# Gated linear attention and a GELU feed-forward: late state products in four corners of the array

## The chip, the cores and the metric

The kernel runs on one core of one Trainium2 chip. The metric is device time in microseconds (us) of one execution. TensorE (PE) multiplies matrices and loads their stationary operand with a separate instruction (PEld in the profile); VectorE (DVE) and ScalarE (ACT) do elementwise work; GpSimd (POOL) does some of it and issues DMAs; SyncE (SP) only issues DMAs. Matmuls write to PSUM, a memory of 128 partitions and eight banks; everything else lives in SBUF.

## The reference

A gated linear attention runs over 4 batches, 8 heads and 768 steps with 48 values per head, and its result goes through a feed-forward layer:

```python
for t in range(S):
    state = alpha[:, :, t, :, None] * state + np.einsum('bhd,bhe->bhde', k[:, :, t], v[:, :, t])
    y[:, :, t] = np.einsum('bhd,bhde->bhe', q[:, :, t], state)
x = y.transpose(0, 2, 1, 3).reshape(3072, 384)
h = x @ w_in                                    # 384 x 2048
out = (0.5 * h * (1 + erf(h / sqrt(2)))) @ w_out  # 2048 x 384
```

## The kernel before

**Tiling.** The 3072 rows are cut into 12 groups of 256 steps (`NG`), three per batch. Attention of a group is done in two units, u = 0 and 1 (`NU`), so there are 24 units. A unit holds four heads: i = 0, 1 picks a pair, and h = 0, 1 picks the head of the pair, which sits in partitions 0 to 47 (h = 0) or 64 to 111 (h = 1). Its 256 steps are four chunks of 64 steps, j = 0 to 3, also written j = 2c + b. Even chunks (b = 0) and odd chunks (b = 1) have separate PSUM banks: the tile `ybank` is 128 partitions by 2 banks, the second index is b.

**A unit in order.** `ahead` (L247) makes decay products on DVE and scales q and k. `scores` (L284) and `turned` (L293) multiply q with k and transpose k; `turned_out` and `masked` take these out of PSUM. `inside` (L322, L340) adds to `ybank` each chunk's own part of the result and each chunk's new state. `chain` (L359) adds the states up from chunk to chunk on DVE. `outside_part` (L384) then adds to the result in `ybank` the product of each chunk's starting state with its q: 16 small products of 48 partitions by 48 columns against 64 steps, for every chunk, pair and head. A unit that begins a batch has no starting state for j = 0 and does 12 of the 16. Then `x_high` (L426) takes the result out on ACT, rounded to fp32r, and `x_low` (L430) writes the remainder on DVE; both go through `x_parts` (L409), which yields for each instruction its source in `ybank` and its two targets. For u = 0 that is one part, for u = 1 two (one into the tile `z`, which `spread` then copies into the last rows of `x` by six DMAs on SP's queue, and one into `x`).

**Where the small products lie in the array.** The partitions of the inputs fix the half of the array's rows that a product uses, and the partitions of the output fix the half of its columns. In `outside_part` both are given by h: `r` is used for `states`, for `qt` and for `ybank`. `scores` uses row half h with column half b and bank h; the first loop of `inside` uses row half b with column half h and bank b.

**Early and late units.** Groups 0 to 2 (`g < NSB`) are early: their feed-forward runs while the weights are still being converted, and their remainders are made by TensorE (`x_minus`, L435) in place. The other nine groups are late: 18 units, six of which begin a batch (groups 3, 6 and 9).

**Feed-forward.** For every group and each of eight slices f, `gemm1` (L457, 18 matmuls) fills `hp`, `gelus` (L469, L470) runs on ACT, `gelu_low` (L475) on DVE, and `gemm2` (L496, 12 matmuls) adds to `acc`; `evacuate` copies `acc` out at the end of a group.

**The order.** Nothing is reordered at run time: the order on PE, DVE, ACT and SP is laid down beforehand by a small planner (L608 to L885). Each step is an `Op` with an engine, a cost from the table `COST`, the steps that it depends on and a rank; the planner runs through time and takes for each free engine the ready step of lowest rank. A step that frees or fills a buffer is simply one of the dependences. Late `scores`, `inside` and `outer` (the step that calls `outside_part`) may be taken only `MARGIN` = 1.5 us after their inputs are ready in the plan, or when no feed-forward step can run, so PE fills with feed-forward work in between. In `plan_unit`, `xh` depends on `outer`, `xl` on `xh`, and the next unit's `inside` on both, since it overwrites `ybank`:

```python
    scan=1.62, back=2.05, q=1.35, qv=0.62, scores=1.2, kn=0.6, mask=0.62, inside=1.2, chain=1.15, outer=0.85, carry=0.26,
    xh=0.6, xl=0.65, spread=0.62, check=0.95, load=0.46, fetch=0.46, u=0.92, c0=0.56, c1=0.9, c2=0.45, c3=0.95, c4=0.92,
```

Of the kernel before, what the change touches and what calls it, by code (L numbers as in the profile page):

```python
# [33 lines left out]
    xh=0.6, xl=0.65, spread=0.62, check=0.95, load=0.46, fetch=0.46, u=0.92, c0=0.56, c1=0.9, c2=0.45, c3=0.95, c4=0.92,  # L34
    hi=0.84, lo=0.9, gemm1=2.12, gelu=0.58, minus=0.35, low=0.63, gemm2=2.1, part=1.1,
# [5 lines left out]
def gla_then_gelu_ffn(ctx: ExitStack, tc: tile.TileContext, q, k, v, alpha, akq, w_in, w_out, out):  # L41
    nc = tc.nc
    B, H, D, S = q.shape
# [5 lines left out]
    CS = C // 2  # L49
    NCH = G // CS  # L50
# [251 lines left out]
    def masked(g, u):  # L302
# [6 lines left out]
            op=ALU.mult,  # L309
        )  # L310

    def inside(g, u):
        d = cur[g, u]
        vn = vbuf[g % NB]
        for i in range(2):
            for j in range(NCH):
                c, b = j // 2, j % 2
                r, t = slice(b * CS, (b + 1) * CS), (2 * i + c) * CS
                for h in range(2):
                    o = slice(h * DP, (h + 1) * DP)  # L320
                    e = (4 * u + 2 * i + h) * D
                    nc.tensor.matmul(  # L322
                        ybank[o, b, t : t + CS],
                        lhsT=vn[r, c, e : e + DP],
                        rhs=d["ss"][r, h, 2 * i + c, :],
                        start=(i == 0 and c == 0),
                        stop=(j == 0 and g % GPB == 0),
                        skip_group_check=True,
                    )
        for j in range(NCH):  # L330
            if ends_batch(g, j):
                continue
            c, b = j // 2, j % 2
            r = slice(b * CS, (b + 1) * CS)
            for i in range(2):
                t = 2 * C + (2 * i + c) * D
                for h in range(2):
                    o = slice(h * DP, (h + 1) * DP)
                    e = (4 * u + 2 * i + h) * D
                    nc.tensor.matmul(  # L340
                        ybank[o, b, t : t + D],
                        lhsT=d["kn"][r, i, c * P + h * DP : c * P + (h + 1) * DP],
                        rhs=vn[r, c, e : e + D],
                        start=False,
                        stop=True,
                        skip_group_check=True,
                    )
# [24 lines left out]

    def outside_part(g, u):
        d = cur[g, u]
        for jj in range(NCH):
            for i in range(2):
                for h in range(2):
                    j = jj ^ h
                    if g % GPB == 0 and j == 0:
                        continue  # L380
                    r = slice(h * DP, h * DP + D)
                    c, b = j // 2, j % 2
                    t = (2 * i + c) * CS
                    ins = nc.tensor.matmul(  # L384
                        ybank[r, b, t : t + CS],
                        lhsT=states[u][j][r, i],
                        rhs=d["qt"][r, i, j * CS : (j + 1) * CS],
                        start=False,
                        stop=True,
                        skip_group_check=True,  # L390
                    )
                    tc.add_manual_dep(
                        ins.ins,
                        d["chain"].ins.name,
                        mybir.DependencyInfo(mybir.DependencyClass.Sync, mybir.DependencyReason.DATA),
                        reason="row tiles of one bank",
                    )
# [11 lines left out]
    def x_parts(g, u):  # L409
        x = cur[g, "x"]  # L410
        y = ybank[:, :, : 2 * C].rearrange("p b (i c t) -> p i c b t", c=2, t=CS)
        if 2 * u + 2 <= NK:
            parts = [(x[:, 2 * u : 2 * u + 2], y)]
        else:
            parts = [(cur[g, "z"].unsqueeze(1), y[:, 1:]), (x[:, NK - 1 : NK], y[:, :1])]
        for to, src in parts:
            hi, lo = (to[:, :, i].rearrange("p i (c b t) -> p i c b t", b=2, t=CS) for i in range(2))
            yield src, hi, lo

    def x_high(g, u):  # L420
        if u == 0:
# [6 lines left out]
    def x_low(g, u):  # L428
        for y, hi, lo in x_parts(g, u):
            nc.vector.tensor_tensor(out=lo, in0=y, in1=hi.bitcast(F32), op=ALU.subtract)  # L430
# [206 lines left out]
    def op(*args, **kw):  # L637
        ops.append(Op(*args, **kw))
        return ops[-1]
# [4 lines left out]
    def plan_unit(n):  # L644
        g, u = divmod(n, NU)
        d = unit[n] = {}
        p, pp_ = unit.get(n - 1, {}), unit.get(n - 2, {})
        r = unit_rank[n]
        fns = {}

        def start():
            fns["f"], fns["q"], fns["b"] = ahead(g, u)
            fns["f"]()

        old = unit.get(n - NB * NU, {})
        used = [old.get(k) for k in ("outer", "scores", "c0", "c1")]
        row = P * 2 * G * 4
        if n < NU:
            d["load"] = op("SP", "load", lambda: load_data(g, u, 0, 1), rank=-40.0 + n, moves=(row,))
            d["rest"] = op("SP", "load", lambda: load_data(g, u, 1, 3), rank=-39.5 + n, moves=(2 * row,))  # L660
        else:
            d["load"] = d["rest"] = op("SP", "load", lambda: load_data(g, u), used, rank=r - 30, moves=(3 * row,))
        if u == 0:
            used = [unit.get(n - NB * NU + i, {}).get("inside") for i in range(NU)]
            d["v"] = op("SP", "load", lambda: load_v(g), used, rank=-38.0 if n < NU else r - 29.5, moves=(P * 2 * H * D * 4,))
        else:
            d["v"] = p["v"]
        d["scan"] = op("DVE", "scan", start, [d["load"], p.get("q"), p.get("back")], rank=r)
        e, cost = ("DVE", "qv") if g < NSB else ("POOL", "q")
        d["q"] = op(e, cost, lambda: fns["q"](), [d["scan"], d["rest"]], rank=r)  # L670
        d["back"] = op("DVE", "back", lambda: fns["b"](), [d["scan"], d["rest"]], rank=r)
        
        
        d["scores"] = op("PE", "scores", lambda: (scores(g, u), turned(g, u)), [d["back"], d["q"], p.get("mask"), p.get("kn")], rank=r)
        d["kn"] = op("ACT", "kn", lambda: turned_out(g, u), [d["scores"], p.get("inside")], rank=-1)
        d["mask"] = op("DVE", "mask", lambda: masked(g, u), [d["scores"], p.get("inside")], rank=-1)
        d["inside"] = op("PE", "inside", lambda: inside(g, u), [d["mask"], d["kn"], d["v"], p.get("xh"), p.get("xl"), p.get("chain"), p.get("outer")], rank=r)
        for side in range(2):
            d["c%d" % side] = op("ACT", "check", lambda side=side: range_check(g, u, side), [d["mask"]], rank=200 + n)
        d["chain"] = op("DVE", "chain", lambda: chain(g, u), [d["inside"], pp_.get("carry")], rank=-1)  # L680
        d["outer"] = op("PE", "outer", lambda: outside_part(g, u), [d["chain"]], rank=r)
        if n < 4:
            for what in ("scores", "inside", "outer"):
                d[what].cost *= SLOW
        for what in ("scores", "inside", "outer"):
            d[what].late = g >= NSB
        d["carry"] = op("DVE", "carry", lambda: carry(g, u), [d["outer"]], rank=0.5)
        free = []
        if g % (XB + 1) == XB and g == XB:
            free = [wops[2 * NF2 - 1]["lo"], wops[2 * NF2 - 1]["hi"]]  # L690
        elif g >= XB + 1:
            free = [("x", g - XB - 1)]
        d["xh"] = op("ACT", "xh", lambda: (to_late(g, u), x_high(g, u)), [d["outer"]], rank=-1)
        d["free"] = free if u == 0 else []
        if g < NSB:
            d["xm"] = op("PE", "minus", lambda: x_minus(g, u), [d["xh"]], rank=-1)
            d["xl"] = op("ACT", "xh", lambda: x_rest(g, u), [d["xm"]], rank=-1)
        else:
            d["xl"] = op("DVE", "xl", lambda: x_low(g, u), [d["xh"]], rank=-0.5)
        if u == NU - 1:  # L700
            part = P * 2 * G
            sides = (("SP", nc.sync, (0,)), ("ACT", nc.scalar, (1,))) if g < NSB else (("SP", nc.sync, (0, 1)),)
            ready_x[g] = [
                op(e, "spread", lambda q=q, hs=hs: spread(g, hs, q), [d["xl"]], rank=-5, moves=(part // 4,) * (NK * len(hs)))
                for e, q, hs in sides
            ]
# [252 lines left out]
```

## Time and profile before

| what | value |
|---|---|
| median of 3 runs | 534.9 us (534.61 to 537.7) |
| profiled execution, its own time | 533.34 us |
| its span, first to last instruction | 531.8 us |
| mean granted TensorE clock | 0.976 |
| PE busy | 510.3 us (96%) |
| DVE busy | 284.3 us (53%) |
| ACT busy | 207.8 us (39%) |
| POOL busy | 33.1 us (6%) |

All durations below are from the profiled execution; 1.5 us of its time lie outside its span. A product in fp32 stands in the trace as two records, each a weight load (PEld) and a matmul (PE), so a full `outside_part` is 32 of each. Matmuls are pipelined and their ends are modelled, so the pace of a block is read from the starts of its weight loads: a line of the timeline gives the start of the first, the time until the end of the last, and their count.

### The profile page before, as it was taken

What the parts mean: (1) busy time and instruction counts of PE and PEld (TensorE: products, weight loads), DVE (VectorE), ACT (ScalarE), POOL (GpSimd) and SP (SyncE); (2) the same over time, 40 slices, a digit from 0 to 9 for tenths busy, and PEclk for the clock granted to TensorE, in tenths of its full rate; (3) what the DMA queues carried; (4) which work ended last, traced back from release to release, by engine and by line L of the source; (5) the groups of instructions that cost most, each with busy time, mean ns of one, the idle gap of its engine ahead of it and who ended that gap; (6) DMA issues with size and microseconds to landing.
All of it is one profiled execution on the core that took longest, in us unless ns stands there. A gap on an engine that the chain in (4) does not pass through costs nothing.

```text
span 531.8 us, 13722 instructions
## 1 busy us (share of the span) xinstructions
PE 510.3 (96%) x5994; PEld 492.8 (93%) x5994; DVE 284.3 (53%) x543; ACT 207.8 (39%) x408; POOL 33.1 (6%) x45
## 2 busy tenths in 40 slices
PE   6689899989999999999999999999999999999995
PEld 6578889989999999999999999999999999999995
DVE  6999999998846655767565435242231121211211
ACT  2566766555433433444333333333222222222221
POOL 1000010000001100201010000000000000000000
PEclk9559999999999999999999999999999999999999
DMA  8856463422024323232242031000000000000001
GB/s 305 319 195 210 139 220 113 128 95 85 2 77 143 101 102 104 92 106 93 87 167 77 1 108 30 1 33 16 1 32 15 1 30 1 31 0 1 31 2 35
DMA packets 15249, 44.20 MB, mean 83 GB/s; under 512 B 2224, under 2 KB 5728, under 8 KB 15184
## 3 DMA queue, kind: packets, MB, share of 16 engines
q1 hardware_dynamic: 13520, 38.44, 22.0%
q0 software_dynamic: 1232, 4.33, 2.2%
q8 instruction: 49, 0.80, 0.6%
q10 hardware_dynamic: 432, 0.49, 0.3%
q14 instruction: 16, 0.13, 0.1%
HBM read 36.18 MB, written 4.72 MB: 77 GB/s over the span
## 4 chain that ended last, share of the span: by engine, by line
PE 83%; DVE 11%; issue 2%; DMA 1%; ACT 1%; SPq 0%; ACTq 0%; DVEq 0%
PE hp L457 36%; PE acc L496 35%; PE ybank L384 3%; PE ybank L322 2%; PE s L293 2%; PE s L284 2%; PE ybank L340 2%; DMA st<-in_moe_w_in_dram 1%; DVE w L193 1%; DVE st L224 1%; DVE u L187 1%; DVE pp L256 1%; DVE rp L265 1%; DVE state L359 1%; DVE u L206 1%
## 5 line engine op out<-in xcount | busy, mean ns | idle before, releaser
L457 PE MATMUL hp<-x,wih 128*128 128x256 f32 x1152 | 214.2, 286 | 0.0
L457 PEld LDWEIGHTS hp<-x,wih 128*128 128x128 f32 x1152 | 183.0, 192 | 1.5 <-PE acc L496 0.3
L457 PE MATMUL hp<-x,wil 128*128 128x256 f32 x576 | 163.4, 284 | 0.0
L475 DVE TENSOR_TENSOR glo<-hp,ghi 128x512 fp32r<-128x512 f32 x86 | 59.3, 690 | 173.4 <-ACT hp L470 172.6
L469 ACT ACTIVATE ghi<-hp 128x512 fp32r<-128x512 f32 x96 | 57.5, 599 | 227.8 <-PE hp L457 224.2
L496 PE MATMUL acc<-woh,ghi 128*128 128x384 f32 x384 | 130.9, 341 | 1.8 <-ACT part L513 1.8
L496 PE MATMUL acc<-wol,ghi 128*128 128x384 f32 x384 | 128.6, 335 | 0.0
L457 PEld LDWEIGHTS hp<-x,wil 128*128 128x128 f32 x576 | 110.8, 192 | 0.0
L496 PE MATMUL acc<-woh,glo 128*128 128x384 f32 x384 | 82.1, 334 | 0.0
L496 PEld LDWEIGHTS acc<-woh,ghi 128*128 128x128 f32 x384 | 72.4, 189 | 2.4 <-ACT part L513 2.0
L496 PEld LDWEIGHTS acc<-wol,ghi 128*128 128x128 f32 x384 | 72.5, 189 | 0.1
L496 PEld LDWEIGHTS acc<-woh,glo 128*128 128x128 f32 x384 | 68.0, 188 | 0.0
L470 ACT ACTIVATE hp<-hp 128x512 f32<-128x512 f32 x96 | 57.1, 595 | 0.0
L256 DVE TENSOR_TENSOR_SCAN pp<-akq,top 128x256 f32<-128x256 f32 x48 | 30.5, 677 | 31.1 <-DMA akq<-in_akq_dram 31.1
L261 POOL TENSOR_TENSOR akq<-akq,pp 128x512 f32<-128x512 f32 x18 | 23.3, 1293 | 212.0 <-DVE pe L257 172.3
L265 DVE TENSOR_TENSOR_SCAN rp<-akq,rp,top 128x255 f32<-128x255 f32 x48 | 34.6, 763 | 0.0
L384 PEld LDWEIGHTS ybank<-akq,state 48*48 48x48 f32 x704 | 22.2, 125 | 9.3 <-DVE state L359 5.1
L384 PE MATMUL ybank<-akq,state 48*48 48x64 f32 x704 | 25.9, 225 | 4.5 <-DVE state L359 4.5
L300 ACT COPY kn<-s 128x512 f32<-128x512 f32 x24 | 14.1, 587 | 38.8 <-PE ybank L340 33.6
L359 DVE TENSOR_TENSOR state<-ybank,state 128x96 f32<-128x96 f32 x80 | 20.5, 256 | 11.8 <-PE ybank L340 9.6
L521 POOL DMA_DIRECT2D out_dram<-part x11 | 8.3, 752 | 250.0 <-DVE part L515 197.0
L322 PEld LDWEIGHTS ybank<-ss,vn 64*64 64x64 f32 x768 | 14.2, 141 | 9.6 <-issue 3.2
(67 smaller groups left out, 401.8 us busy)
## 6 DMA issues: line engine op xcount, KB each, us to landing
akq<-in_akq_dram SPq DMA_DIRECT2D x22, 768.0 KB, 5.2
st<-in_moe_w_in_dram SPq DMA_DIRECT2D x8, 768.0 KB, 4.4
st<-in_moe_w_out_dram SPq DMA_DIRECT2D x8, 768.0 KB, 4.3
vn<-in_v_dram SPq DMA_DIRECT2D x12, 384.0 KB, 3.5
out_dram<-part POOLq DMA_DIRECT2D x11, 384.0 KB, 3.4
x<-z SPq DMA_DIRECT2D x63, 32.0 KB, 3.2
akq<-in_akq_dram SPq DMA_DIRECT2D x2, 512.0 KB, 4.9
akq<-in_akq_dram SPq DMA_DIRECT2D x2, 256.0 KB, 3.9
```

What stands on the lines that cost most here:

```text
L256: nc.vector.tensor_tensor_scan(pp[:, i], at[:, i], top, MID, ALU.mult, ALU.min)
L261: (nc.vector if g < NSB else nc.gpsimd).tensor_tensor(out=qt, in0=qt, in1=pp, op=ALU.mult)
L265: nc.vector.tensor_tensor_scan(rp[:, i, G - 2 :: -1], at[:, i, G - 1 : 0 : -1], top[:, 1:], rp[:, i, G - 1 :], ALU.mult, ALU.min)
L300: nc.scalar.copy(d["kn"], d["s"][:, :, 2 * C : 4 * C])
L322: nc.tensor.matmul(ybank[o, b, t : t + CS], lhsT=vn[r, c, e : e + DP], rhs=d["ss"][r, h, 2 * i + c, :], start=(i == 0 and c == 0), stop=(j ...
L359: d["chain"] = nc.vector.tensor_tensor(out=st[j + 1], in0=new, in1=st[j], op=ALU.add)
L384: ins = nc.tensor.matmul(ybank[r, b, t : t + CS], lhsT=states[u][j][r, i], rhs=d["qt"][r, i, j * CS : (j + 1) * CS], start=False, stop=Tru ...
L457: nc.tensor.matmul(hp[:, j, :], lhsT=a[:, j, i * P : (i + 1) * P], rhs=x[:, i, :], start=(j == 0 and i == 0 and n == 0), stop=(i == NK - 1 ...
L469: nc.scalar.activation(ghi, hp, AF.Gelu)
L470: nc.scalar.activation(hp, hp, AF.Gelu)
L475: nc.vector.tensor_tensor(out=glo, in0=hp, in1=ghi.bitcast(F32), op=ALU.subtract)
L496: nc.tensor.matmul(acc[t], lhsT=a[:, j, t * C : (t + 1) * C], rhs=w[:, j, :], start=(first and j == 0 and k == 0 and w is wo_hi[f]), stop= ...
```

## The change

For late units, the results of odd chunks (b = 1) of head h are written to the other partition half of `ybank`. `inside` (first loop) and `outside_part` both follow this. The order of the products in `outside_part` becomes: c, then i, then the four combinations of b and h; for early units b is exchanged with h as before. `x_parts` yields for late units the even chunks in one part and the odd chunks in two parts of 64 partitions, each read from one half of `ybank` and written to the other half of its target; so `x_high` and `x_low` issue three instructions where they issued one (u = 0), and six where they issued two (u = 1). In the planner the cost of late `outer` goes from 0.85 to 0.6, and that of late `xh` and `xl` from 0.6 and 0.65 to 1.15 (u = 0) or 1.6 (u = 1). Early units keep their halves, their parts and their costs.

```diff
+    def turned_over(g, b):
+        return g >= NSB and b == 1
+
     def inside(g, u):
@@
                 for h in range(2):
-                    o = slice(h * DP, (h + 1) * DP)
+                    o0 = (h ^ turned_over(g, b)) * DP
+                    o = slice(o0, o0 + DP)
                     e = (4 * u + 2 * i + h) * D
                     nc.tensor.matmul(
                         ybank[o, b, t : t + CS],
@@ def outside_part(g, u):
-        for jj in range(NCH):
+        for c in range(NCH // 2):
             for i in range(2):
-                for h in range(2):
-                    j = jj ^ h
+                for bb, h in ((0, 0), (0, 1), (1, 0), (1, 1)):
+                    b = bb if g >= NSB else bb ^ h
+                    j = 2 * c + b
                     if g % GPB == 0 and j == 0:
                         continue
                     r = slice(h * DP, h * DP + D)
-                    c, b = j // 2, j % 2
+                    o0 = (h ^ turned_over(g, b)) * DP
+                    o = slice(o0, o0 + D)
                     t = (2 * i + c) * CS
                     ins = nc.tensor.matmul(
-                        ybank[r, b, t : t + CS],
+                        ybank[o, b, t : t + CS],
                         lhsT=states[u][j][r, i],
                         rhs=d["qt"][r, i, j * CS : (j + 1) * CS],
@@ def x_parts(g, u):
-            yield src, hi, lo
+            if g < NSB:
+                yield src, hi, lo
+                continue
+            yield src[:, :, :, 0], hi[:, :, :, 0], lo[:, :, :, 0]
+            for h in range(2):
+                r, o = slice(h * DP, (h + 1) * DP), slice((1 - h) * DP, (2 - h) * DP)
+                yield src[o, :, :, 1], hi[r, :, :, 1], lo[r, :, :, 1]
@@ def plan_unit(n):
             d["xl"] = op("DVE", "xl", lambda: x_low(g, u), [d["xh"]], rank=-0.5)
+            d["outer"].cost = 0.6
+            d["xh"].cost = d["xl"].cost = 1.15 if u == 0 else 1.6
```

## Rows read from the trace of the kernel before

**Rows 1.** Busy time in one stretch: length, engines, PE clock, DMA share, GB/s.

```profile
140.00:400.00 260.00, 260.00 (x3535) 251.05 (x3534) 130.07 (x278) 96.68 (x204) 22.91 (x21) 1.00 0.22 70
```

The engines in Rows 1 are, in this order, PE, PEld, DVE, ACT and POOL, with the count of instructions in brackets.

**Rows 2.** Groups by line and shape, 86 to 400 us: busy, mean ns | idle before.

```profile
L384 PEld LDWEIGHTS ybank<-akq,state 48*48 48x48 f32 x528 | 15.8, 120 | 3.6 <-issue 1.5 <-DVE glo L475 0.5 <-DVE akq L268 0.3
...
L322 PEld LDWEIGHTS ybank<-ss,vn 64*64 64x64 f32 x544 | 9.5, 134 | 3.5 <-DVE glo L475 1.5 <-issue 1.2
L430 DVE TENSOR_TENSOR x<-ybank,x 128x512 fp32r<-128x512 f32 x9 | 6.1, 681 | 0.0
L426 ACT CAST x<-ybank 128x512 fp32r<-128x512 f32 x9 | 5.3, 590 | 0.9 <-PE ybank L384 0.9
```

**Rows 3.** Timeline of weight loads, a late full block of 32, no scores behind.

```profile
365.28 0.95 PEld L384 LDWEIGHTS ybank<-akq,state 48*48 48x48 f32 x32
366.31 0.19 PEld L496 LDWEIGHTS acc<-woh,ghi 128*128 128x128 f32 x1
```

**Rows 4.** Timeline of weight loads, a late block of 24 that begins a batch.

```profile
86.56 0.73 PEld L384 LDWEIGHTS ybank<-akq,state 48*48 48x48 f32 x24 [0.25 <-issue]
87.37 0.30 PEld L457 LDWEIGHTS hp<-x,wih 128*128 128x128 f32 x2
```

**Rows 5.** Timeline of weight loads, scores by themselves, then both loops of inside.

```profile
75.25 0.56 PEld L284 LDWEIGHTS s<-akq 48*64 48x64 f32 x32 [0.25 <-issue]
75.88 0.20 PEld L293 LDWEIGHTS s<-ident,akq 128*128 128x128 f32 x2
...
200.31 0.56 PEld L322 LDWEIGHTS ybank<-ss,vn 64*64 64x64 f32 x32 [0.25 <-issue]
200.77 0.55 PEld L340 LDWEIGHTS ybank<-vn,kn 64*64 64x64 f32 x24
201.37 0.30 PEld L457 LDWEIGHTS hp<-x,wih 128*128 128x128 f32 x2
```

**Rows 6.** Timeline of weight loads, blocks of 32 and 24 with scores behind.

```profile
250.85 0.94 PEld L384 LDWEIGHTS ybank<-akq,state 48*48 48x48 f32 x31 [0.25 <-issue]
...
252.34 0.42 PEld L293 LDWEIGHTS s<-ident,akq 128*128 128x128 f32 x4
...
156.48 0.73 PEld L384 LDWEIGHTS ybank<-akq,state 48*48 48x48 f32 x24
...
157.76 0.31 PEld L293 LDWEIGHTS s<-ident,akq 128*128 128x128 f32 x3
```

**Rows 7.** Timelines of ACT and of DVE around taking out x.

```profile
157.60 0.38 ACT L426 CAST z<-ybank 128x256 fp32r<-128x256 f32 x1
157.86 0.38 ACT L426 CAST x<-ybank 128x256 fp32r<-128x256 f32 x1
160.62 0.60 ACT L469 ACTIVATE ghi<-hp 128x512 fp32r<-128x512 f32 x1 [2.37 <-PE hp L457]
...
158.32 0.41 DVE L430 TENSOR_TENSOR z<-ybank,z 128x256 fp32r<-128x256 f32 x1
158.65 0.41 DVE L430 TENSOR_TENSOR x<-ybank,x 128x256 fp32r<-128x256 f32 x1
161.74 0.69 DVE L475 TENSOR_TENSOR glo<-hp,ghi 128x512 fp32r<-128x512 f32 x1 [2.67 <-ACT hp L470]
...
265.32 0.68 DVE L430 TENSOR_TENSOR x<-ybank,x 128x512 fp32r<-128x512 f32 x1
266.60 0.56 DVE L515 COPY part<-acc 128x384 f32<-128x384 f32 x1 [0.60 <-PE acc L496]
```

**Rows 8.** Timeline of DVE and PEld where the next inside follows soonest.

```profile
316.96 0.41 DVE L430 TENSOR_TENSOR x<-ybank,x 128x256 fp32r<-128x256 f32 x1
...
318.99 0.56 PEld L322 LDWEIGHTS ybank<-ss,vn 64*64 64x64 f32 x32 [0.25 <-issue]
```

**Rows 9.** Timeline of SP and PEld: spread of group 3, and its first gemm1.

```profile
158.76 3.67 SPq L449 DMA_DIRECT2D x<-z  x6
...
170.05 0.30 PEld L457 LDWEIGHTS hp<-x,wih 128*128 128x128 f32 x2
```

## The prediction, made blind

> **What bounds the kernel now.** I read the busy times by stretch first, then the groups by line, then timelines of single engines around the late units. From 140 to 400 us PE is busy for 260.00 of 260.00 us, at full granted clock, while DVE has 130 and ACT 97 [rows 1]. Seventeen of the eighteen late `outside_part` blocks lie in that stretch, the other one at 86.56 [rows 4]. So in this stretch the time is the sum of PE's work: microseconds taken from PE arrive at the end one for one, and work added to DVE and ACT costs something only where PE comes to wait for it. The order on PE is fixed, but feed-forward steps fill it between the attention steps, so a shorter attention step simply moves everything behind it forward.
>
> **The state products now.** Late blocks hold 528 records [rows 2]: 12 full blocks of 32, and 6 blocks of 24 that begin a batch. A full block of 32 loads lasts 0.95 us, one load 0.12, so the starts are (0.95 - 0.12) / 31 = 26.8 ns apart [rows 2, 3]. `scores` and the first loop of `inside`, also 32 loads, last 0.56 us; with 0.134 for one load that is 13.7 ns apart [rows 2, 5]. The code gives the reason: `outside_part` uses two corners of the array (row half h with column half h), the two others use all four. Per corner both keep nearly the same pace, 2 x 26.8 = 54 ns and 4 x 13.7 = 55 ns. The corners work side by side, and one corner takes a record every 55 ns or so, whatever the others do.
>
> **What the change gives on PE.** Late blocks now use row half h with column half h in bank 0, and with the other column half in bank 1: four corners, 8 records each where two had 16.
> A full block by itself: 365.28 to 366.31 is 1.03 us to the next work [rows 3]. The same 32 records in four corners took 75.25 to 75.88, 0.63 us [rows 5]. Gain 0.40.
> A full block with scores behind it: 250.85 to 252.34, 1.49 us [rows 6]. In its place a four-corner block running into the next, 0.46 us from start to start (200.31 to 200.77), and 0.63 for the scores [rows 5]: 1.09. Gain 0.40.
> A block of 24: 86.56 to 87.37, 0.81 us [rows 4]. After the change its odd corners have 8 records and its even ones 4, the unequal filling that the second loop of `inside` has when it has 24: 200.77 to 201.37, 0.60 us [rows 5]. Gain 0.21. With scores behind it: 156.48 to 157.76, 1.28 us [rows 6], against 1.09: gain 0.19.
> Of the 12 full blocks 10 have scores behind them, of the 6 short ones 5. Sum: 12 x 0.40 + 5 x 0.19 + 0.21 = 4.80 + 0.95 + 0.21 = **5.96 us**.
> No row shows 48-column loads in four corners. The upper bound is the 54 ns of today's corner instead of 55 to 58: 8 x 3 ns, or 0.02 us a block, 0.4 us in all, so 6.4 us. The lower bound is no gain at all (first rival). I take the rows of `scores`, which have the same 48 rows and the same four corners. Turning the odd results in `inside` costs nothing on PE: the same four corners in another order. For early units the new order still alternates between two corners, as now.
>
> One thing speaks against full speed. In the new order two products in different row halves run at once into one bank. Today's full blocks avoid this by pairing bank 0 with bank 1. But a block of 24 has it already: with j = 0 left out, the first four records of either corner go to the odd bank, h = 1 in the upper corner and h = 0 in the lower. Taken in turns they would need four more steps of 54 ns, 0.22 us; the block of 24 lasts 0.73 us, which is (0.73 - 0.12) / 23 = 26.5 ns a record [rows 4], the pace of the full block. So the trace shows no turn-taking where column halves differ, and they differ in the new pairs too.
> The Trainium skill, TensorEngine Tiling (Array Packing), section Restrictions and Gotchas, states that different row tiles cannot access the same PSUM bank simultaneously and that software must see to it. By that rule the new pairs would run in turn and nothing would be gained; the block of 24 disagrees, so its weight here is that of the first rival.
>
> **What the change adds on ACT and DVE.** Per late group one instruction becomes three (u = 0) and two become six (u = 1), on either engine: 27 become 81. The trace has no copy of 64 partitions and none that moves data to the other half; I price them by columns, as if they had 128 partitions. u = 0: three of 256 columns, ACT 3 x 0.38 = 1.14 for 0.59, DVE 3 x 0.41 = 1.23 for 0.68 [rows 2, 7]. u = 1: six of 128 columns. On the line through 512 and 256 columns these are 0.38 - (0.59 - 0.38) / 2 = 0.27 us on ACT and 0.41 - (0.68 - 0.41) / 2 = 0.28 on DVE, so 1.64 and 1.65. Now they take 157.60 to 158.24, 0.64, and 158.32 to 159.06, 0.74 [rows 7]. Added: about 0.55 (u = 0) and 1.0 (u = 1) on each engine. That is the upper bound; these instructions overlap, 0.26 us from start to start for 0.38 of length [rows 7], and at such spacing it is about half.
> What hides it: behind `xh` on ACT stand range checks, the copy of `kn` and the next gelu; the gelu follows after 2.37 us idle at the tightest. Behind `xl` on DVE the next remainder of a gelu, which `gemm2` waits for, follows after 2.67 us idle. One copy of partial sums (265.32) has 0.60 us, enough for a u = 0 unit's 0.55 [rows 7]. The next `inside` waits for `xl` too: at the tightest `xl` ends at 317.37 and `inside` starts at 318.99, 1.62 us later [rows 8]. The x of group 3 sets out at 158.76, and the first `gemm1` that reads it starts at 170.05; the six DMAs start over 3 us and land 3.67 us or less after, by about 165.5 [rows 9], so 1.5 us later is still 3 us early. Loads for later units stand behind these DMAs on SP's queue and would start as much later, with the same room. I take 0. Without the cover, PE would wait the excess over these gaps; for all 18 units at 1.0 us over it would be 18 us.
>
> **The planner's new costs** change no duration, only the order: some feed-forward and attention steps may change places. A place matters for PE in one way: where scores stand directly behind the state products the array keeps its form. Apart, the two blocks take 1.03 + 0.63 = 1.66 us instead of 1.49, and a second entry of 0.25 us idle [rows 3, 5, 6]: 0.42 for a separation. Both steps become ready at about the same time as now, so I take 0 and keep up to six separations, 2.5 us, for the range.
>
> **Sum.** 533.34 - 5.96 = 527.4 us for an execution like the profiled one, which is 1.56 us below the median of the runs. On the median's scale 534.9 - 6.0 = **528.9 us**.
>
> **Rivals.**
> First, the two row halves take turns in a bank. A full block then runs two records at a time, 1.03 us as today. A short block has eight records in the odd bank in turn: 8 x 54 ns = 0.43, sixteen more at 26.8 ns = 0.43, and 0.20 until the next work: 1.06 against 0.81, six times 0.25 = 1.5 us. Time 534.9 + 1.5 = 536.4 us. For: today's order of full blocks. Against: the block of 24. Chance 0.07.
> Second, the order comes apart: three to all fifteen pairs separated, or PE waiting for a late `xl`, 1.3 to 6.3 us given back, 530.2 to 535.2 us. For: many small shifts of cost in the planner. Against: the gaps above. Chance 0.13.
> Third, slower: the array empties between row halves in one bank. After a block the last load starts 0.12 before its end, 366.11, and the next work, of another form, at 366.31, 0.20 us later [rows 3]. At that price a full block has two such turns in each of four rounds, 1.6 us more, a short one six, 1.2. Less the gain, 12 x (1.6 - 0.40) + 6 x (1.2 - 0.2) = 20.4: 555 us. It decides from 0.40 / 8 = 0.05 us a turn. Against: the same block of 24, and `scores`, which changes halves at every record at 13.7 ns [rows 5]. Chance 0.05.
>
> **How the numbers follow.** The forecast holds with 0.75, within 527.4 to 530.4 (gain 4.5 to 7.5, the bounds of the pace and small shifts of order). To 533.5 it takes in about half of the second rival; the first, the third and the rest of the second, about 0.18 with what lies below, stay out. Range **527.4 to 533.5**. A measurement of this kernel tells about 1% from no change, so 529.6 us is the border: the forecast lies only 0.7 us below it. Faster by over 1%: 0.75 of the forecast's 0.75, or 0.56. Within 1%: the rest of it, 0.19, the first two rivals, 0.18: 0.37. Slower: the third and what is left, 0.07.
>
> **What would show it.** Right: late L384 blocks of 32 loads in about 0.56 us at 13.5 to 14.5 ns, of 24 in about 0.55; PE still full from 140 to 400 us; ACT and DVE up by 7 to 14 us each. Wrong: L384 at 26 ns (first rival), L284 with idle time or a block of its own in late units (second), loads 0.05 us or more apart (third).

## The result, and the profile after

The changed kernel takes 528.19 us (median of four runs, 527.54 to 529.19); the kernel before, beside it, 535.33 us. The ratio is 0.9876 with an interval of 0.9847 to 0.9905: faster by 1.2%, 5 to 8 us. The profiled execution takes 527.96 us, where the one of before took 533.34: 5.4 us less. Forecast were 528.9 us, and 527.4 for an execution like the profiled one.

First the state products. In the changed kernel line 384 is line 390, 322 is 326, 340 is 344, 457 is 469, 469 is 481, 475 is 487, 496 is 508 and 513 is 525. Three stretches of the timeline of weight loads (start, time to the end of the last, count): a full block by itself, a short one, a full one with scores behind it. They answer to [rows 3, 4, 6].

```profile
363.43 0.52 PEld L390 LDWEIGHTS ybank<-akq,state 48*48 48x48 f32 x32 [0.25 <-issue]
364.02 0.19 PEld L508 LDWEIGHTS acc<-woh,ghi 128*128 128x128 f32 x1
...
86.33 0.50 PEld L390 LDWEIGHTS ybank<-akq,state 48*48 48x48 f32 x24 [0.25 <-issue]
86.91 0.30 PEld L469 LDWEIGHTS hp<-x,wih 128*128 128x128 f32 x2
...
250.01 0.52 PEld L390 LDWEIGHTS ybank<-akq,state 48*48 48x48 f32 x32
250.44 0.56 PEld L284 LDWEIGHTS s<-akq 48*64 48x64 f32 x32
251.07 0.31 PEld L293 LDWEIGHTS s<-ident,akq 128*128 128x128 f32 x3
```

The full block went from 1.03 to 0.59 us (363.43 to 364.02), the short one from 0.81 to 0.58, the full one with its scores from 1.49 to 1.06 (250.01 to 251.07). The records of a full block start (0.52 - 0.12) / 31 = 12.9 ns apart instead of 26.8.

Next the stretch that was full before, with the engines in the order of [rows 1], and then, from 86 to 400 us, the groups that take x out of PSUM (line 426 became 438, and 430 became 442): busy us and mean ns, then idle time.

```profile
140.00:400.00 260.00, 259.60 (x3571) 250.00 (x3570) 151.00 (x337) 112.10 (x262) 22.90 (x21) 1.00 0.23 71
```

```profile
L442 DVE TENSOR_TENSOR x<-ybank,x 64x256 fp32r<-64x256 f32 x18 | 7.6, 421 | 0.2
L438 ACT CAST x<-ybank 64x256 fp32r<-64x256 f32 x18 | 6.6, 367 | 0.2
L442 DVE TENSOR_TENSOR x<-ybank,x 64x128 fp32r<-64x128 f32 x18 | 5.2, 288 | 0.4
...
L438 ACT CAST x<-ybank 64x128 fp32r<-64x128 f32 x18 | 4.7, 260 | 0.3
...
L442 DVE TENSOR_TENSOR x<-ybank,x 128x256 fp32r<-128x256 f32 x9 | 3.8, 423 | 6.3 <-ACT x L438 6.3
L438 ACT CAST x<-ybank 128x256 fp32r<-128x256 f32 x9 | 3.4, 376 | 6.4 <-PE ybank L390 6.4
```

PE is still full, all but 0.4 us. DVE did 21 us more in this stretch and ACT 15 us. A copy of 64 partitions costs what one of 128 does (0.367 against 0.376 us on ACT). Reading one partition half into the other makes no single instruction longer, but it costs something where the instructions follow each other. Below are the three instructions of a u = 0 unit on ACT and on DVE, first in the changed kernel, then in the first experiment, which leaves every result in its own half:

```profile
221.58 1.13 ACT L438 CAST x<-ybank 128x256 fp32r<-128x256 f32 x3
222.75 1.30 DVE L442 TENSOR_TENSOR x<-ybank,x 128x256 fp32r<-128x256 f32 x3 [0.26 <-ACT x L438]
...
223.67 1.00 ACT L438 CAST x<-ybank 128x256 fp32r<-128x256 f32 x3
224.71 1.19 DVE L442 TENSOR_TENSOR x<-ybank,x 128x256 fp32r<-128x256 f32 x3
```

In the changed kernel the second of the three starts on ACT 0.39 us after the first, which lasts 0.377, so they do not overlap; with the halves left alone it starts after 0.26 us. A u = 1 unit takes 1.67 us on ACT and 1.86 on DVE, with the halves left alone 1.43 and 1.64.

**Where the time went.** Take every weight load from the first late state product on (86.56 us before, 86.33 after; the loads ahead of it are equal in number), and add up by line the time until the start of the next load, up to the last load. The late state products have 14.22 us before and 8.06 after: 6.16 us less. The loads of `gemm1` have 199.68 and 201.49: 1.81 us more. Those of `gemm2` stay the same (188.56 and 188.61), and the others together change by 0.2 us. The whole went from 438.90 to 434.34 us, 4.56 us less. The rest of the 5.4 us lies outside: 0.24 us ahead of this stretch and 0.59 us after the last weight load. That last part is no work of PE's, and its cause is open; from the last load to the end of the span the two kernels that take x out in the old parts have 6.29 and 6.44 us, the eight runs of kernels with the new parts 5.70 to 5.82.

So a part of the gain on the state products was given back in waits that stand behind `gemm1` and inside `gemm2`. Two of them are not in the profile of before; the timeline of weight loads shows them.

```profile
117.97 0.19 PEld L469 LDWEIGHTS hp<-x,wil 128*128 128x128 f32 x1
119.07 0.19 PEld L508 LDWEIGHTS acc<-woh,ghi 128*128 128x128 f32 x1 [0.90 <-ACT ghi L481]
...
273.82 0.19 PEld L508 LDWEIGHTS acc<-wol,ghi 128*128 128x128 f32 x1
274.73 0.19 PEld L508 LDWEIGHTS acc<-woh,glo 128*128 128x128 f32 x1 [0.72 <-DVE glo L487]
```

The first stands in a second profile of the changed kernel too (`e5_changed_again` below: 0.89 us at 120.69). The second does not, so it does not come from the order alone. In all, the same stretch takes 433.25 us there: two executions of one kernel differ by 1.1 us in it, and a difference of that size between two profiles shows little.

And two of the fifteen pairs of state products and scores came apart. Here is one, 2.86 us from start to start with feed-forward work between its halves, and a second entry of 0.25 us:

```profile
220.46 0.50 PEld L390 LDWEIGHTS ybank<-akq,state 48*48 48x48 f32 x24
...
223.32 0.56 PEld L284 LDWEIGHTS s<-akq 48*64 48x64 f32 x32 [0.25 <-issue]
```

### The profile page after: what moved, and what is told of

It reads as the page before. It is cut to its first block, busy times and chain, and to the rows that moved or that the text cites. A ratio compares the mean times of both kernels' runs of the same rounds, so it can differ in the third digit from the quotient of the medians.

```text
span 526.4 us, 13851 instructions
## 1 busy us (share of the span) xinstructions
PE 504.8 (96%) x5994; PEld 487.1 (93%) x5994; DVE 303.9 (58%) x599; ACT 221.4 (42%) x462; POOL 33.1 (6%) x45
## 4 chain that ended last, share of the span: by engine, by line
PE 80%; DVE 13%; DMA 3%; issue 2%; ACT 1%; SPq 0%; DVEq 0%; ACTq 0%
PE hp L469 35%; PE acc L508 35%; PE ybank L390 2%; DVE rp L265 2%; PE ybank L326 2%; PE s L293 2%; PE s L284 2%; DVE pp L256 2%; PE ybank L344 2%; DMA st<-in_moe_w_in_dram 1%; DVE w L193 1%; DMA akq<-in_akq_dram 1%; DVE st L224 1%; DVE u L187 1%; DVE state L363 1%
## 5 line engine op out<-in xcount | busy, mean ns | idle before, releaser
L265 DVE TENSOR_TENSOR_SCAN rp<-akq,rp,top 128x255 f32<-128x255 f32 x48 | 39.0, 852 | 0.2
L390 PEld LDWEIGHTS ybank<-akq,state 48*48 48x48 f32 x704 | 15.6, 125 | 9.1 <-DVE state L363 5.1
L442 DVE TENSOR_TENSOR x<-ybank,x 64x256 fp32r<-64x256 f32 (+3 forms) x54 | 19.2, 356 | 7.2 <-ACT x L438 6.3
L390 PE MATMUL ybank<-akq,state 48*48 48x64 f32 x704 | 19.3, 228 | 4.2 <-DVE state L363 4.2
L438 ACT CAST x<-ybank 64x256 fp32r<-64x256 f32 (+4 forms) x60 | 19.9, 332 | 7.1 <-PE ybank L390 6.4
```

Source lines behind the costliest of these rows:

```text
L265: nc.vector.tensor_tensor_scan(rp[:, i, G - 2 :: -1], at[:, i, G - 1 : 0 : -1], top[:, 1:], rp[:, i, G - 1 :], ALU.mult, ALU.min)
L390: ins = nc.tensor.matmul(ybank[o, b, t : t + CS], lhsT=states[u][j][r, i], rhs=d["qt"][r, i, j * CS : (j + 1) * CS], start=False, stop=Tru ...
L438: nc.scalar.copy(hi, y)
```

## The experiments

Two theories stood against each other. One: the gain is the four corners on PE, and the new order, which the three planner costs bring about, gives back between one and two us. The other: part of the gain is the order, or the taking out of x, not the corners. The runs below were all measured beside the kernel before; the ratios are to that.

### The four corners undone

```diff
     def turned_over(g, b):
-        return g >= NSB and b == 1
+        return 0
@@ def x_parts(g, u):
-                r, o = slice(h * DP, (h + 1) * DP), slice((1 - h) * DP, (2 - h) * DP)
+                r = o = slice(h * DP, (h + 1) * DP)
```

> The changed kernel with its odd results left in their own half: same order of every engine, same three parts of x, the same planner costs, but the state products lie in two corners again. Theory (the gain is the four corners on PE): the late state product blocks go back from 8.1 us to about 14.2 us in all, PE is never idle between 140 and 400 us, so 6.1 us longer than the changed kernel: 534 us on the scale where the changed kernel has 528.2. Rival (the gain comes from the new order or the new costs): within 2 us of the changed kernel, 528 to 530.

Measured: 534.62 us, ratio 0.9996 (0.9979 to 1.0014). The gain is gone. The order of the instructions on all engines is that of the changed kernel, and so are the three parts. The block that took 0.59 us, in the timeline of weight loads of this run:

```profile
368.51 0.95 PEld L390 LDWEIGHTS ybank<-akq,state 48*48 48x48 f32 x32 [0.25 <-issue]
369.54 0.19 PEld L508 LDWEIGHTS acc<-woh,ghi 128*128 128x128 f32 x1
```

It has its 1.03 us of [rows 3] again. Added up by line, the late state products take 14.55 us, where the changed kernel has 8.06 with the same order: 6.5 us. From the first late state product to the last load it is 440.03 us against 434.34 and 433.25 in the two profiles of the changed kernel, 5.7 and 6.8 us; the ratios (0.9996 against 0.9876 and 0.9879) make it 6.3 us. So nearly all of what the corners save arrives at the end.

### The new costs by themselves

```diff
 (kernel before)
             d["xl"] = op("DVE", "xl", lambda: x_low(g, u), [d["xh"]], rank=-0.5)
+            d["outer"].cost = 0.6
+            d["xh"].cost = d["xl"].cost = 1.15 if u == 0 else 1.6
```

> The kernel before with only the planner's three costs changed. Theory (the costs give nothing and their order brings new waits of PE, 0.9 us at 118 us and 0.7 us at 274 us in the changed kernel, and separates two pairs of blocks at 0.42 us each): 0 to 2.5 us longer than before, 535 to 538 on the scale where before has 535.3. Rival (a better order is part of the gain): 2 us or more shorter than before.

Measured: 536.53 us, ratio 1.0025 (1.0004 to 1.0046): 0.2 to 2.5 us slower, as the theory has it; the order is no part of the gain. What it costs is less certain. Eight of the twelve executions had a mean granted clock of 0.969 to 0.972 and took 536.0 to 537.9 us, the other four 534.2 to 534.7; of the 22 of the kernel before, five had 0.968 or less and took 535.9 to 537.2. A part of the 1.3 us between the medians may be the clock. The two separated pairs are there, and the wait at 118 us too. These are the longest waits of PE's loads from 86 us on (total, times, longest); the one of 0.9 put down to "issue" is that at 118 us:

```profile
PEld ybank L322 <- DVE glo L475: 1.5, 6, 0.3
PEld ybank L384 <- issue: 1.5, 6, 0.2
PEld acc L496 <- ACT part L513: 1.0, 1, 1.0
PEld acc L496 <- issue: 0.9, 1, 0.9
```

The wait for the copy of partial sums (L513) went the other way. It was twice as long before:

```profile
PEld acc L496 <- ACT part L513: 2.0, 1, 2.0
```

From the first late state product to the last load this run takes 439.69 us, 0.8 more than before: two separations of 0.4 us and 0.9 us at 118, less 1.0 us of this wait. The run with the corners undone has the same order and three parts where this one has one, and takes 440.03 us, 0.3 more. Both differences are smaller than the 1.1 us between two profiles of one kernel. So the separations and the waits can be seen one by one, but neither what the order costs in all nor a cost of the added copies stands clear of that.

### The old costs with the new layout

```diff
 (changed kernel)
-            d["outer"].cost = 0.6
-            d["xh"].cost = d["xl"].cost = 1.15 if u == 0 else 1.6
```

> The changed kernel with the planner's old costs, so the order of before; everything else as changed. Theory (the waits that took back 1.6 us and the separated pairs come from the order): those waits are gone, state product blocks still 8.1 us in all, so 1 to 2 us shorter than the changed kernel, 526 to 527.2. Rival (the waits come from the longer taking out of x, whatever the order): as the changed kernel or up to 2 us longer, since the planner now places x too early.

Measured: 529.58 us, ratio 0.9911 (0.9879 to 0.9942). It was not 1 to 2 us shorter; whether it is longer than the changed kernel can't be told, since the intervals overlap. My expectation fell: the order of before is not the better one for the new kernel. All fifteen pairs are together again and the late state products take 7.58 us, but the waits of PE's loads from 86 us on begin with a new one:

```profile
PEld ybank L326 <- DVE x L442: 2.3, 3, 0.9
PEld acc L508 <- ACT part L525: 2.0, 1, 2.0
```

In three units the next `inside` waits for `xl`, 2.3 us in all. The planner, told 0.6 and 0.65, put it too early: these `inside` blocks start 0.05 us after `xl` ends. In the kernel before the three tightest distances were 1.59 to 1.64 us, and in the changed kernel, whose planner was told, they are 1.60 to 1.68. So the added copies are hidden because the planner was told of them. (The profiled execution of this run had 10 us more at the lower granted clock, at 50 to 56 and 118 to 121 us, so its sums aren't compared.)

### The taking out doubled

```diff
 (changed kernel)
         for y, hi, _ in x_parts(g, u):
-            nc.scalar.copy(hi, y)
+            for _ in range(2 if g >= NSB else 1):
+                nc.scalar.copy(hi, y)
@@ def x_low(g, u):
+            for _ in range(2):
                 nc.vector.tensor_tensor(out=lo, in0=y, in1=hi.bitcast(F32), op=ALU.subtract)
```

> The changed kernel with every copy and every subtraction that takes late x out of PSUM done twice, which repeats work and changes no value; planner costs as changed. It adds about 14 us or more to ACT and 19 us to DVE. Theory (idle time of 2.4 us ahead of the next gelu covers it): a pair of takings out grows by 0.8 to 1.6 us an engine and unit, PE waits in few places, 0 to 2 us longer than the changed kernel, 528.2 to 530.2. Rival (the added work of the change is already at the edge of its cover): PE waits in most of the 18 late units, 5 us or more longer.

Measured: 546.67 us, ratio 1.0227 (1.0197 to 1.0257): 18 us longer than the changed kernel. Here the rival was right. The waits of PE's loads from 140 us on (in this kernel and the next, lines from `x_low` on stand two further down):

```profile
PEld ybank L326 <- DVE x L444: 10.8, 12, 2.3
PEld acc L510 <- DVE glo L489: 5.8, 6, 1.5
PEld ybank L390 <- DVE state L363: 2.5, 4, 1.6
```

Twelve of the `inside` blocks wait for x. The idle 2.4 us ahead of the next gelu does not protect PE: most of the loss comes where the distance from `xl` to the next `inside` has run out.

### The same, with the planner told

```diff
 (the doubled kernel)
-            d["xh"].cost = d["xl"].cost = 1.15 if u == 0 else 1.6
+            d["xh"].cost = d["xl"].cost = 2.3 if u == 0 else 3.2
```

> The kernel that takes late x out twice, but with the planner told of it: costs of late xh and xl 2.3 (u = 0) and 3.2 (u = 1) instead of 1.15 and 1.6. The untold one took 546.7, 18 us more than the changed kernel, with 12 waits of inside for x, 10.8 us, and 6 waits of gemm2 for the remainder of a gelu, 5.8 us. Theory (the cover is what the planner puts between xl and the next inside, not idle time as such): the waits of inside are gone, 3 to 8 us of others stay: 531 to 536. Rival (ACT and DVE have no room for the doubled work, wherever it stands): 540 or more.

Measured: 538.87 us, ratio 1.007 (1.0043 to 1.0097): between the two forecasts. Told, the planner takes away 8 of the 18 us. The rest stays; of the waits of PE's loads from 86 us on the first two are these:

```profile
PEld ybank L326 <- DVE x L444: 7.3, 7, 2.2
PEld acc L510 <- DVE glo L489: 3.3, 2, 2.5
```

Seven blocks still wait for x. In the eight u = 1 units with an `inside` behind them it starts 0.05 or 0.06 us after `xl` ends; there the doubled steps take 3.44 us on ACT and 3.80 on DVE, and the planner was told 3.2 for each. So it was told too little where it waits. Whether the measured costs would take the waits away wasn't tried, so the rival, that ACT and DVE have no room for this work, stays open.

### The changed kernel again, and banks in runs

The changed kernel, unaltered, was run again beside the next two.

> The changed kernel again, unaltered, so that the three beside it share its chip and its runs of the kernel before: 0.985 to 0.991 of before.

Measured: 528.92 us, ratio 0.9879 (0.9849 to 0.991).

For late units, the order of the state products with b outermost:

```diff
-        for c in range(NCH // 2):
-            for i in range(2):
-                for bb, h in ((0, 0), (0, 1), (1, 0), (1, 1)):
+        fine = [(c, i, bb, h) for c in range(2) for i in range(2) for bb in range(2) for h in range(2)]
+        runs = [(c, i, bb, h) for bb in range(2) for c in range(2) for i in range(2) for h in range(2)]
+        for c, i, bb, h in fine if g < NSB else runs:
...
```

> The changed kernel with the state products of late units in another order: first all of bank 0, then all of bank 1, so that for 16 records at a time only two corners are asked for, and both row halves write one and the same bank. Theory (a corner takes a record every 55 ns and the engine looks only a few records ahead): two corners at a time again, late blocks 13 to 14.5 us in all instead of 8.1, about 5 to 6 us longer than the changed kernel. Theory of far lookahead: 8 to 10 us in all, at most 1 us longer. Rival (row halves take turns in a bank): 53 ns a record, a full block 1.7 us, late blocks about 27 us in all and the kernel some 19 us longer.

Measured: 531.9 us, ratio 0.9937 (0.9914 to 0.996), 3.0 us longer than the changed kernel beside it: between the two theories of lookahead, and far from the rival. The timeline of weight loads of a full block (line 390 is 392 here, 508 is 510), first whole, then as it is seen in a window that ends at 365.79:

```profile
365.53 0.78 PEld L392 LDWEIGHTS ybank<-akq,state 48*48 48x48 f32 x32 [0.25 <-issue]
366.38 0.19 PEld L510 LDWEIGHTS acc<-woh,ghi 128*128 128x128 f32 x1
...
365.53 0.34 PEld L392 LDWEIGHTS ybank<-akq,state 48*48 48x48 f32 x10 [0.25 <-issue]
```

In the first 0.26 us ten records start. All of them go to bank 0, by turns from the upper and the lower row half. Their starts stand in pairs 7 ns apart, and from pair to pair it is 42 ns once and then 55, two corners at full pace. Taking turns in the bank would have let half as many start. Then, between 365.79 and 365.82, four start, and so on for three rounds; after that it is two at a time again. The first record of bank 1 is the 17th in order, and since each bank has 16 records, it is among the four that start once ten have started. So the engine looks about five records ahead in this block. The order that is laid down beforehand is that of the steps; among the records inside a step, PE starts some ahead of their turn. And an order that goes round the corners is a part of the gain: late state products 10.21 us instead of 8.02, and the scores behind them 11.63 instead of 10.54, probably since the last corners are still busy when they come.

### Costs in between, and the second loop round the corners

In the changed kernel, costs between the old and the new ones keep all fifteen pairs together in the plan, and the second loop of `inside`, which works in row half 0 for eight records and then in row half 1, can go round the corners too:

```diff
-            d["xh"].cost = d["xl"].cost = 1.15 if u == 0 else 1.6
+            d["xh"].cost = d["xl"].cost = 1.05 if u == 0 else 1.4
@@ def inside(g, u), second loop
-        for j in range(NCH):
+        for c, i, b in ((c, i, b) for c in range(2) for i in range(2) for b in range(2)):
+            j = 2 * c + b
...
```

> The changed kernel with late xh and xl at 1.05 (u = 0) and 1.4 (u = 1) in the planner, by which all fifteen pairs of state products and scores stay together, and with the second loop of inside in the order c, i, b, so that its products go round the four corners too. Theory: two separations less, 0.8 us, and the second loop from 15.4 to about 13.6 ns a record in its full blocks, 12 x 0.05 = 0.6 us in the late units: 1.0 to 2.5 us shorter than the changed kernel beside it, if the order brings no new wait. Rival: the shorter costs bring waits of inside for x, as the old costs did (2.3 us): as the changed kernel or longer.

Measured: 526.72 us (525.95 to 527.63), ratio 0.9844 (0.9814 to 0.9875), against 528.92 (527.5 to 529.34) of the changed kernel beside it: 2.2 us, within the forecast, though the two intervals to the kernel before overlap. Added up by line, late state products take 7.58 us (8.02 there), the second loop 10.42 (10.94), and no `inside` waits for x. The wait at 118 us is still there, 0.9 us. The whole stretch from the first late state product on is 1.0 us shorter (432.24 against 433.25); the other 1.2 us are not traced, and the two edits were not tried one by one.

## Why the prediction was right

**PE is the bound, and its work counts one for one.** Right. Undoing the corners alone gave the whole gain back, 5.7 and 6.8 us by the two profiles of the changed kernel and 6.3 by the ratios.

**The price of the blocks.** Right, and a little too low. For full blocks 0.40 was forecast, 0.44 by itself and 0.43 with scores were measured; for short ones 0.21 and 0.19 against 0.23 and, by the same reading of the other short blocks, 0.23. With the order held the same they make 6.5 us (14.55 to 8.06), where the sum had 5.96 and its upper bound 6.4. The reason for the difference is the one kept for the upper bound: in these blocks a corner takes a record each 56 ns also when four are in use, where the rows of `scores`, which were taken, have 58.

**Row halves in one bank.** Right: the block of 24 had shown it, and the run with banks in runs shows it for ten records in a row. The Trainium skill, TensorEngine Tiling (Array Packing), section Restrictions and Gotchas, has row tiles unable to use one bank at the same time; in this run they do, at 55 ns a record and corner, with their column halves apart. Row halves of one bank in the same column half were not tried.

**The added copies.** The length of one was right: 0.27 and 0.28 us were forecast for 128 columns, about 0.26 and 0.29 measured. That they overlap was wrong. The prediction counted 1.14 and 1.64 us on ACT, 1.23 and 1.65 on DVE as an upper bound; measured from the first start to the last end it is 1.13 and 1.67, 1.29 and 1.86, since the turned halves do not overlap. ACT's total rose by 13.6 us. DVE's rose by 19.6, outside the 7 to 14 that were named as a sign: 13.4 of it is taking x out, and 4.4 are backward scans that became slower (below).

That the copies cost nothing was right in the result, and the reason was only half right. The prediction set about 1.0 us against each gap by itself. But `xl` follows `xh`, so for the next `inside` both additions count: in a u = 1 unit 1.02 us on ACT (1.67 instead of 0.65) and 1.10 on DVE (1.86 instead of 0.76), 2.1 us together, more than the 1.62 us of [rows 8] (the tightest was 1.59, at 358.12). With the old costs this cover is indeed gone in three units; it is there in the changed kernel because the planner's new costs, named as a mere change of order, put the next `inside` later. The price named for a lost cover, 18 us, is what the doubled run cost, but by another sum: 12 waits for x and 6 for a remainder, not a fixed excess in each unit.

**The order.** The term that was taken as 0 is about 0.8 us in the profile of the new costs by themselves. The separations that the prediction had named are there, two of them at 0.4 us; the wait of `gemm2` for a late gelu, 0.9 us, was not named, nor that a wait for the copy of partial sums would be 1.0 us shorter. All of it lay in the range (up to 2.5 us).

So the number came out well partly by luck: the better pace (0.5 us more than forecast) and the cost of the order (0.8 us more) nearly cancel, and 0.6 us came after the last weight load, which the prediction did not speak of. 5.96 us were forecast, 5.4 measured between the two profiled executions, 7.1 between the medians and 6.1 when it was run again, with 5 to 8 as interval.

## What to carry to other kernels

Small products that use only the two corners on the diagonal can be moved by turning half of the outputs to the other partition half; it pays when the order of issue goes round all four, and when the engines that read the result have time to turn it back. Before counting a longer copy as hidden, look for the first later step on the bound engine that waits for it, not for the next idle time on the copying engine, and add up what grows on every engine along that path. In a kernel with an order laid down beforehand, a new cost for one step is a change of its own, to be tried by itself.

## What the runs showed of the hardware

Backward scans on DVE slow down when POOL multiplies beside them. In the changed kernel's timeline, unfiltered around 271 us:

```profile
270.85 1.31 POOL L261 TENSOR_TENSOR akq<-akq,pp 128x512 f32<-128x512 f32 x1 [9.69 <-DVE pe L257]
...
271.05 2.30 DVE L265 TENSOR_TENSOR_SCAN rp<-akq,rp,top 128x255 f32<-128x255 f32 x2
```

The pair of scans takes 2.30 us, 1.65 for the first of them, where scans that stand free take 0.73 each; POOL's multiply takes its 1.3 us as always. The new order put eight scans beside a multiply of 1.3 us, the old one three, and the mean of the 48 scans rose from 763 to 852 ns; with the old costs and the new layout it is two scans and 760 ns. The remainder that PE waited for at 274 us stands behind this pair on DVE. But the second profile of the changed kernel has the same slow pair (2.26 us) without that wait. What differs is the step ahead of it, a scan that waits for a load; first the changed kernel's profile, then the second one:

```profile
269.33 1.28 DVE L256 TENSOR_TENSOR_SCAN pp<-akq,top 128x256 f32<-128x256 f32 x2 [2.14 <-DMA akq<-in_akq_dram]
...
270.00 1.27 DVE L256 TENSOR_TENSOR_SCAN pp<-akq,top 128x256 f32<-128x256 f32 x2 [1.19 <-DMA akq<-in_akq_dram]
```

So the slow scans alone did not make PE wait there; the load of `akq` came 0.95 us later against the work around it.
